# Queries written once and spread into zeroed halves by DMA, with a new table of planning rules, in a fused attention and MLP kernel

## The chip, the cores and the metric

The kernel runs on one core of one Trainium2 chip. The metric is device time in microseconds for one execution. The kernel before has a median of 776.76 us over three runs (775.57 to 777.45).

## The reference, cut to what matters

Two branches read the same x of 2048 rows by 512 columns and are mixed by a gate per row. Branch A is attention with 32 heads of 16 columns. Branch B is an MLP with two layer norms and a shift of four column groups along the rows.

```python
def _A_ref(x, wqkv, wo):                      # B=1, S=2048, D=512, H=32, Dh=16
    q, k, v = split(x @ wqkv)
    scores = jnp.einsum("bhqd,bhkd->bhqk", q, k) * (Dh ** -0.5)
    o = jnp.einsum("bhqk,bhkd->bhqd", _softmax(scores), v)
    return merge(o) @ wo
def _B_ref(x, w1, w2, w3, w4):
    x1 = x + shifted(_gelu(_layernorm(x) @ w1)) @ w2
    return x1 + _gelu(_layernorm(x1) @ w3) @ w4
g = _sigmoid((x * gate_w).sum(-1, keepdims=True))
return g * a + (1 - g) * b
```

The exponentials of the scores are most of the work: 32 heads of 2048 x 2048.

## The kernel before, in words

**Tiles.** Queries are taken in four chunks c of 512 columns (CH). The heads go in eight units u of four heads for each chunk, 32 units in all. A unit holds 64 score blocks: 16 tiles of 128 keys times four heads, and one block is 128 keys by 512 queries. That makes 2048 blocks.

**Queries and the mask.** One product with wq gives a tile ps_q of 128 rows: eight heads of 16 rows, that is two units. A score product takes 32 rows, the keys of two neighbouring heads. So that only one of the two counts, the query tile qT has two halves, each [128, 512]: half a keeps the rows of the heads with number a in their pair, and has zeros in the other rows. In `q_proj` (line 313) the tile is made by one VectorE product of ps_q, read twice, with a mask column for each half (line 321). The mask also holds the factor QS. There are 16 such tiles; the first, for chunk 0 and heads 0 to 7, is made in four pieces at the start (lines 1350 to 1373), the other 15 at line 321.

**Two ways to an exponential.** A score block goes one of two ways. On the first, two or three blocks stand in one PSUM tile `stage`, and ScalarE turns them into probabilities `pt` in one instruction (line 1076, in `expo`). On the second, VectorE dumps a block from the PSUM tile `dsc` as 16-bit integers (line 959, in `whole`), and four blocks of one key tile, a group, are then shifted four times as integers (VectorE line 1000, or GpSimd line 998). The five integer tiles, read as bf16, add up to the exponential. TensorE then multiplies the probabilities with V (line 1089, in `attend_block`), once for a block of the first way, five times for one of the second, and sums in `acc`. The tiles of the second way are named quad, more or xT, after the buffers that they stand in.

**The end of a unit.** `finish_unit` (line 1164) copies acc to the single buffer `accsb` (VectorE, line 1171), moves the denominators by a DMA (den, line 1179), takes reciprocals (line 1186), writes them to DRAM and reads them back spread over rows (rec_d and bcs, lines 1187 and 1188), multiplies on GpSimd (oT, line 1201), and copies the result's rows into a dense tile by four DMAs (line 1210). All these DMAs stand on SyncE's queue (SP), which takes them one by one in the order in which they are written down.

**What sets the order.** The program is a planner that is run when the kernel is built: it keeps a clock of its own for each engine, and writes the instructions down in the order in which they come by that clock. `wants_whole` decides before each score tile whether a block goes to VectorE. Its limits come from `rule`, which looks in a table RULES for the current unit: NEED and AHEAD (how near the end of a unit the next one may start), DLIM (how much VectorE may have waiting), CHAINS (groups open at once), MAXD (the most score blocks of a unit that may go to VectorE). PTS and MANY decide when products with V go ahead of other products. Where TensorE has nothing to do by that clock, `fill` writes products with zeros.

**The last unit.** Its end is cut into ranges of query tiles, j = 0 and 1, j = 2, j = 3. For each j, `out` (line 1290) makes the product with wo. For j = 0 ScalarE and then GpSimd finish the tile (lines 1306 and 1309), for the others VectorE does (line 1299). In the list of TensorE's waiting work a lower number goes first.

Of the kernel before, what the change touches and what calls it, by code (L numbers as in the profile page):

```python
# [12 lines left out]
ALU = mybir.AluOpType  # L13
AX = mybir.AxisListType
BF16 = mybir.dt.bfloat16
# [17 lines left out]
def kernel(  # L33
# [13 lines left out]
    nc = tc.nc  # L47
    P = 128
# [4 lines left out]
    DH = D // H  # L53
# [3 lines left out]
    PTB = 6  # L57
# [5 lines left out]
    CH = 512  # L63
# [18 lines left out]
    qpool = ctx.enter_context(tc.tile_pool(name="qpool", bufs=2))  # L82
# [9 lines left out]
    ptE = young.enter_context(tc.tile_pool(name="ptE", bufs=8))  # L92
# [72 lines left out]
    MM = 0.214  # L165
# [49 lines left out]
    def dma(t, own, count=1):  # L215

        state["sp"] = max(state["sp"], t) + own * count
        return state["sp"]
# [80 lines left out]
    def k_proj(G, c):  # L299
        yield all_at(("xT", c), ("wk", G > 0))  # L300
        ps = gen("ps_k")
        yield from proj(ps, wkv, slice(G * P, (G + 1) * P), xT[c])

        def fn(end):
            nc.vector.tensor_copy(out=kT[G][:, c, :], in_=ps[:])
            at["k", G, c] = end

        evac(0.69, fn)
        yield MM

    qTs = {}

    def q_proj(c, G):
        yield all_at(("xT", c), ("wq", G > 0), ("qfree", NU // 2 * c + G - 2))
        ps = gen("ps_q")
        yield from proj(ps, wq, slice(G * P, (G + 1) * P), xT[c])

        def fn(end):
            qT = qpool.tile([P, 2, CH], BF16, tag="qT", name="qT")
            qTs[(c, G)] = qT  # L320
            nc.vector.tensor_tensor(out=qT[:], in0=ps[:].unsqueeze(1).to_broadcast([P, 2, CH]),
                                    in1=mask[:].unsqueeze(2).to_broadcast([P, 2, CH]), op=ALU.mult)
            at["q", c, G] = end

        evac(1.23, fn)
        yield MM
# [703 lines left out]
    def exp_option():  # L1030
        while next_slot["exp"] in lone:
            next_slot["exp"] += 1
        k = next_slot["exp"]
        if k not in scored:
            return None
        t = scored[k]
        if k in turn:
            return turn[k][2]() if turn[k][1] else t
        back, used = (8, young_pts) if k < EARLY else (PTB, late_pts)
        if len(used) >= back:  # L1040
            if used[-back] not in pt_free:
                return None
            t = max(t, pt_free[used[-back]])
        return t
# [482 lines left out]
```

## Time and profile before

| | before |
|---|---|
| median of three runs | 776.76 us |
| the profiled execution's own time | 777.28 us |
| its span, first to last instruction | 775.5 us |
| mean granted TensorE clock | 0.996 |
| exponentials on ScalarE (line 1076) | 687 |
| score dumps of 512 columns from dsc on VectorE (line 959) | 475 |
| shifts on GpSimd (line 998) | 105 |

The page gives the busy time of each engine, the chain of work that ended last, and groups of instructions by line. A group's row reads: line, engine, operation, tiles, shapes, count, then busy time and the mean duration of one in ns, then the idle time of the engine just before them and what ended it. Where instructions of one engine overlap, busy time is less than count times duration. SPq is SyncE's queue of DMAs. In a row of a timeline the first two numbers are the start and the length in us.

### The profile page before, as it was taken

The numbers are of one execution on the slowest core, as the hardware profiler recorded it, in microseconds if no ns is written. First come the engines' busy times: TensorE is split into PE (matmuls) and PEld (weight loads), VectorE is DVE, ScalarE is ACT, GpSimd is POOL, SyncE is SP. The second block draws the span as 40 slices with busy tenths as digits, with TensorE's granted clock in tenths as the row PEclk, the third lists the DMA queues.
The fourth block names the chain that finished last, engine by engine and source line by source line (L and its number), as shares of the span: only waits on it lengthen the run. The fifth ranks groups of instructions, "written<-read, shape, count | busy, mean of one in ns | idle before, by whom it ended". The sixth has DMA issues, their size and how long they took to land.

```text
span 775.5 us, 24000 instructions
## 1 busy us (share of the span) xinstructions
PE 749.0 (97%) x10166; PEld 245.6 (32%) x10166; DVE 718.0 (93%) x1234; ACT 757.7 (98%) x731; POOL 254.3 (33%) x190
## 2 busy tenths in 40 slices
PE   8999999999999999899999999999999999999997
PEld 4334323333333232232223223322332232332233
DVE  5798999999999999899999999999999989999993
ACT  6999999999999999899999999999999999999995
POOL 3221433442313414234442333123323412443420
PEclk9999999999999999999999999999999999999999
DMA  8600012111130005002000013000040000000010
GB/s 209 192 20 17 13 50 64 31 34 42 19 36 19 19 15 127 20 16 47 20 12 27 19 33 44 18 8 19 19 53 21 16 21 25 21 23 19 20 40 28
DMA packets 52307, 29.05 MB, mean 37 GB/s; under 512 B 36712, under 2 KB 47720, under 8 KB 52200
## 3 DMA queue, kind: packets, MB, share of 16 engines
q1 hardware_dynamic: 51240, 27.00, 15.1%
q8 instruction: 79, 1.29, 0.7%
q10 hardware_dynamic: 960, 0.52, 0.2%
q14 instruction: 28, 0.23, 0.1%
HBM read 17.17 MB, written 2.35 MB: 25 GB/s over the span
## 4 chain that ended last, share of the span: by engine, by line
ACT 51%; PE 29%; issue 16%; DVE 2%; DMA 1%; POOL 0%; POOLq 0%; ACTq 0%; DVEq 0%; SPq 0%
ACT pt L1076 47%; PE acc L1089 11%; PE stage L754 9%; PE ps L271 4%; PE ps_y L271 2%; ACT g2T L1053 1%; PE ps_o L271 1%; ACT g2T L1056 1%; ACT hT L1053 1%; DMA bcs<-rec_d 1%; ACT L1053 1%; PE warm L1330 0%; DVE quad L959 0%; DMA rec_d<-rec 0%; DVE quad L1000 0%
## 5 line engine op out<-in xcount | busy, mean ns | idle before, releaser
L1076 ACT ACTIVATE pt<-stage 128x1024 bf16<-128x1024 f32 (+1 forms) x687 | 707.7, 1207 | 4.1 <-PE stage L754 2.6
L754 PE MATMUL stage<-qT,kT 32*128 32x512 bf16 (+1 forms) x1597 | 271.7, 380 | 16.7 <-ACT pt L1076 12.4
L959 DVE TENSOR_SCALAR quad<-dsc 128x512 int16<-128x512 f32 x342 | 227.6, 683 | 13.2 <-PE dsc L754 10.9
L998 POOL TENSOR_SCALAR quad<-quad 128x2048 int16<-128x2048 int16 x71 | 134.9, 1901 | 261.9 <-DVE quad L1000 145.9
L754 PE MATMUL dsc<-qT,kT 32*128 32x512 bf16 x475 | 182.6, 384 | 0.0
L754 PEld LDWEIGHTS <-kT 32*128 32x128 bf16 x2072 | 81.9, 91 | 284.0 <-issue 250.3
L1000 DVE TENSOR_SCALAR quad<-quad 128x2048 int16<-128x2048 int16 x212 | 146.8, 705 | 2.3 <-PE acc L1089 1.9
L1089 PE MATMUL acc<-pt,vp 128*17 128x512 bf16 (+2 forms) x1572 | 147.4, 379 | 1.4 <-DVE accsb L1171 0.7
L1089 PE MATMUL acc<-quad,vp 128*17 128x512 bf16 x1696 | 145.4, 382 | 0.0
L1089 PEld LDWEIGHTS <-vp 128*17 128x17 bf16 (+1 forms) x4072 | 82.7, 89 | 131.1 <-issue 95.5
L271 PE MATMUL ps<-w,g2T 128*32 128x512 bf16 x896 | 70.5, 382 | 0.0
L1201 POOL TENSOR_TENSOR oT<-accsb,bcs 128x512 bf16<-128x512 f32 x29 | 37.1, 1278 | 66.1 <-DVE quad L1000 48.8
L271 PE MATMUL ps_y<-xnT,w 128*32 128x512 bf16 x704 | 56.2, 387 | 1.0 <-DVE accsb L1171 0.8
L959 DVE TENSOR_SCALAR more<-dsc 128x512 int16<-128x512 f32 x77 | 51.2, 681 | 1.8 <-PE dsc L754 1.6
L998 POOL TENSOR_SCALAR more<-more 128x2048 int16<-128x2048 int16 x17 | 32.3, 1900 | 61.2 <-DVE more L1000 31.6
L998 POOL TENSOR_SCALAR xT<-xT 128x2048 int16<-128x2048 int16 x13 | 25.0, 1924 | 69.8 <-DVE quad L1000 31.0
L1089 PE MATMUL acc<-more,vp 128*17 128x512 bf16 x424 | 40.4, 380 | 0.0
L959 DVE TENSOR_SCALAR xT<-dsc 128x512 int16<-128x512 f32 x56 | 37.3, 681 | 2.6 <-PE dsc L754 2.2
L271 PEld LDWEIGHTS <-w 128*32 128x32 bf16 x1152 | 28.0, 96 | 34.3 <-issue 17.2
L1089 PE MATMUL acc<-xT,vp 128*17 128x512 bf16 x380 | 36.0, 383 | 0.0
L271 PE MATMUL acc<-wq,zero 128*32 128x512 bf16 x324 | 29.8, 383 | 0.0
L271 PEld LDWEIGHTS <-g2T 128*32 128x32 bf16 x896 | 19.3, 95 | 22.1 <-issue 14.3
(117 smaller groups left out, 598.4 us busy)
## 6 DMA issues: line engine op xcount, KB each, us to landing
bcs<-rec_d SPq DMA_DIRECT2D x31, 256.0 KB
w<-in_B_w_dram SPq DMA_DIRECT2D x2, 1792.0 KB
out_dram<-ot SPq DMA_DIRECT2D x15, 128.0 KB
x_sb<-in_A_x_dram SPq DMA_DIRECT2D x14, 128.0 KB
oT<-oT SPq DMA_DIRECT2D x112, 16.0 KB
w<-in_B_w_dram SPq DMA_DIRECT2D x2, 512.0 KB
wkv<-in_A_wqkv_dram SPq DMA_DIRECT2D x1, 512.0 KB
wo_all<-in_A_wo_dram SPq DMA_DIRECT2D x8, 64.0 KB
```

The lines of the kernel that those rows point to most:

```text
L271: nc.tensor.matmul(out[j:j + 32, :], lhsT=lhsT[:, j:j + 32], rhs=rhs, tile_position=(0, j), **kwargs)
L754: nc.tensor.matmul(out, lhsT=kT[G][32 * j:32 * j + 32, cc, o:o + P], rhs=qTs[(c, G)][32 * j:32 * j + 32, a, lo:hi], start=True, stop=True, ...
L959: nc.vector.tensor_scalar(out=bits[:, r:r + wide, :], in0=dsc.rearrange("p (a c) -> p a c", c=CH), scalar1=SHIFT, scalar2=LOWEST, op0=ALU. ...
L998: behind(nc.gpsimd.tensor_scalar(out=tiles[to], in0=tiles[base], scalar1=1.0, scalar2=shift, op0=ALU.mult, op1=ALU.add))
L1000: fast["ins"] = nc.vector.tensor_scalar(out=tiles[to], in0=tiles[base], scalar1=shift, scalar2=None, op0=ALU.add)
L1053: nc.scalar.activation(out=part, in_=part, func=ACT.Gelu_apprx_tanh)
L1056: nc.scalar.activation(out=dst, in_=stages.pop(k)[:, 0:len(ms) * CH].rearrange("p (a c) -> p a c", c=CH), func=ACT.Gelu_apprx_tanh)
L1076: nc.scalar.activation(out=pt[:, 0:w], in_=stages.pop(k)[:, 0:w], func=ACT.Exp, scale=LN2 / 128.0)
L1089: nc.tensor.matmul(accs[n][32 * j:32 * j + M, lo:hi], lhsT=lhsT, rhs=p, start=(kt == 0), stop=(kt == NT - 1), skip_group_check=True, tile_ ...
L1201: behind(nc.gpsimd.tensor_tensor(out=oT, in0=tiles["accsb"][:], in1=tiles["bcs"][:], op=ALU.mult))
```

## The change

VectorE now writes the queries once, scaled, into a tile `dense` of [128, 512]. Eight DMAs on SyncE's queue, one for each head, put its 16-row strips into the half that each belongs to. The query tiles are two fixed buffers, qbufs, that take turns. Their other rows stay zero: buffer 1 is cleared by GpSimd at the start, buffer 0 is written with its zeros by the first tile's four pieces. The planner counts the eight DMAs at 0.6 us each, and 2.3 us more, before a score may read the tile. Early pt buffers go from eight to seven. The table RULES differs for 26 of the 31 units that it has; the caps MAXD of units 1 to 31 (20 where a unit names none, and for the last) add up to 540 blocks before and 528 in the change. In the last unit the product of j = 0 goes ahead of other work.

```diff
-    qpool = ctx.enter_context(tc.tile_pool(name="qpool", bufs=2))
+    qpool = ctx.enter_context(tc.tile_pool(name="qpool", bufs=1))
...
-    ptE = young.enter_context(tc.tile_pool(name="ptE", bufs=8))
+    ptE = young.enter_context(tc.tile_pool(name="ptE", bufs=7))
...
-    RULES = {1: {"MANY": 8, "NEED": 32, "WIDE": 1, "AHEAD": 16, "MAXD": 20, "PTS": 6, "CHAINS": 2, "HURRY": 14, "DLIM": 1.2},
+    RULES = {1: {"WIDE": 1, "NEED": 34, "AHEAD": 12, "HURRY": 18, "DLIM": 0.9, "MANY": 8, "PTS": 3, "CHAINS": 6, "MAXD": 16},
...
     qTs = {}
+    qbufs = [const.tile([P, 2, CH], BF16, name=f"qT{i}") for i in range(2)]
+    nc.gpsimd.memset(qbufs[1][:], 0.0)
...
         def fn(end):
-            qT = qpool.tile([P, 2, CH], BF16, tag="qT", name="qT")
-            qTs[(c, G)] = qT
-            nc.vector.tensor_tensor(out=qT[:], in0=ps[:].unsqueeze(1).to_broadcast([P, 2, CH]),
-                                    in1=mask[:].unsqueeze(2).to_broadcast([P, 2, CH]), op=ALU.mult)
-            at["q", c, G] = end
-
-        evac(1.23, fn)
+            dense = qpool.tile([P, CH], BF16, tag="dense", name="dense")
+            nc.vector.tensor_scalar(out=dense[:], in0=ps[:], scalar1=QS, scalar2=None, op0=ALU.mult)
+            qT = qTs[(c, G)] = qbufs[G % 2]
+            for o in range(0, P, DH):
+                nc.sync.dma_start(out=qT[o:o + DH, o // DH % 2, :], in_=dense[o:o + DH, :])
+            at["q", c, G] = dma(end, 0.6, 8) + 2.0 + MARGIN
+
+        evac(0.69, fn)
...
-        back, used = (8, young_pts) if k < EARLY else (PTB, late_pts)
+        back, used = (7, young_pts) if k < EARLY else (PTB, late_pts)
...
-                queue["pe"].append((2 - 3 * r, 2 * MM, lambda begin, j=j: out(j), fits))
+                queue["pe"].append((2 - 3 * r if j else -10, 2 * MM, lambda begin, j=j: out(j), fits))
...
-    qT = qpool.tile([P, 2, CH], BF16, tag="qT", name="qT")
-    qTs[(0, 0)] = qT
+    qT = qTs[(0, 0)] = qbufs[0]
```

The table moves instructions on all engines. Three places are shown. The first is ScalarE at its last exponentials, from some forty of them to the end; "x8" means that eight like it follow one another. Before:

```order
L1076 ACTIVATE pt<-stage 128x1024 x8
L1076 ACTIVATE pt<-stage 128x1536
L1076 ACTIVATE pt<-stage 128x1024 x4
L1076 ACTIVATE pt<-stage 128x1536 x3
L1076 ACTIVATE pt<-stage 128x1024 x8
L1076 ACTIVATE pt<-stage 128x1536 x6
L1076 ACTIVATE pt<-stage 128x512
L1076 ACTIVATE pt<-stage 128x1024 x2
L1076 ACTIVATE pt<-stage 128x1536 x4
```

And ScalarE at the same place of the change:

```order
L1079 ACTIVATE pt<-stage 128x1024 x4
L1079 ACTIVATE pt<-stage 128x1536 x3
L1079 ACTIVATE pt<-stage 128x1024 x12
L1079 ACTIVATE pt<-stage 128x1536 x8
L1079 ACTIVATE pt<-stage 128x1024 x16
L1079 ACTIVATE pt<-stage 128x1536 x8
L1079 ACTIVATE pt<-stage 128x1024 x2
L1079 ACTIVATE pt<-stage 128x1536 x4
```

Wide and narrow exponentials change places here as in most units. Over the whole order there are 511 of 1024 columns, 175 of 1536 and one of 512 before, 491 of 1024 and 194 of 1536 in the change. VectorE's groups of four blocks go from 125 to 121 (500 blocks to 484), and their shifts from 395 on VectorE and 105 on GpSimd to 399 and 85. TensorE's zero products go from 332 to 516.

The second place is SyncE's queue from the first unit's end on. Before:

```order
L1179 DMA den<-accsb 128x1x16
L1187 DMA rec_d<-rec 128x16
L1188 DMA bcs<-rec_d 128x1x512
L1210 DMA oT_252<-oT 16x512 x4
L1179 DMA den<-accsb 128x1x16
L1187 DMA rec_d<-rec 128x16
L1188 DMA bcs<-rec_d 128x1x512
L1210 DMA oT_252<-oT 16x512 x4
L1179 DMA den<-accsb 128x1x16
L1187 DMA rec_d<-rec 128x16
L1188 DMA bcs<-rec_d 128x1x512
```

And SyncE's queue there in the change, with lines three higher:

```order
L1182 DMA den<-accsb 128x1x16
L1190 DMA rec_d<-rec 128x16
L1191 DMA bcs<-rec_d 128x1x512
L325 DMA qT_244<-dense 16x512 x8
L1213 DMA oT_255<-oT 16x512 x4
L1182 DMA den<-accsb 128x1x16
L1190 DMA rec_d<-rec 128x16
L1191 DMA bcs<-rec_d 128x1x512
L1213 DMA oT_255<-oT 16x512 x4
L1182 DMA den<-accsb 128x1x16
L325 DMA qT_243<-dense 16x512 x8
L1190 DMA rec_d<-rec 128x16
```

The first eight query DMAs stand between a unit's bcs and its oT copies, the second eight between a unit's den and its rec_d. The second kind of place is the most frequent of the 15.

The third place is TensorE at the very end, the products of the last unit's ranges. L1263 makes denominators, L1275 spreads reciprocals, and each two products of L1294 make one tile j. Before:

```order
L1275 MATMUL end<-identf,rec 32x128 x8
L1263 MATMUL end<-pick,accsb 128x4
L1275 MATMUL end<-identf,rec 32x128 x8
L1294 LDWEIGHTS oT_256
L1294 MATMUL end<-wo_pad,oT_256 128x512
L1294 LDWEIGHTS oT_257
L1294 MATMUL end<-wo_pad,oT_257 128x512
```

And TensorE's end in the change:

```order
L1266 MATMUL end<-pick,accsb 128x4
L1297 LDWEIGHTS oT_259
L1297 MATMUL end<-wo_pad,oT_259 128x512
L1297 LDWEIGHTS oT_260
L1297 MATMUL end<-wo_pad,oT_260 128x512
L1266 MATMUL end<-pick,accsb 128x4
L1278 MATMUL end<-identf,rec 32x128 x8
L1297 LDWEIGHTS oT_259
```

The tile of j = 0 now stands ahead of the last range's denominators, where before all four tiles stood behind them.

2 lines of the change are left out of this document (1 added, 1 removed).

## The prediction

> **What bounds the kernel now.** I read the busy shares first, then the stretch in which exponentials run, then what the engines waited for.
>
> ```profile
> PE 749.0 (97%) x10166; PEld 245.6 (32%) x10166; DVE 718.0 (93%) x1234; ACT 757.7 (98%) x731; POOL 254.3 (33%) x190
> ACT 51%; PE 29%; issue 16%; DVE 2%; DMA 1%; POOL 0%; POOLq 0%; ACTq 0%; DVEq 0%; SPq 0%
> ```
>
> ScalarE (ACT), TensorE (PE) and VectorE (DVE) are all nearly full, and the chain that ended last runs half over ACT. Which of the three is the floor shows in the busy time between the first exponential (8.68 us) and the end of the last (766.6 us). The first line has all engines (stretch, its length, then busy time of PE, PEld, DVE, ACT, POOL), the second line 1076, the exponential, alone.
>
> ```profile
> 8.68:766.60 757.92, 737.81 (x10066) 239.89 (x10067) 711.63 (x1218) 754.07 (x725) 246.96 (x154) 1.00 0.16 36
> 8.68:766.60 757.92, 707.70 (x687) 1.00 0.16 36
> ```
>
> ACT is busy 754.07 of 757.92 us there, 707.70 in exponentials and 46.4 in GELUs and table loads. Successive exponentials overlap, so the price of one is its pace, from stretches that hold hardly anything but one shape:
>
> ```profile
> L1076 ACT ACTIVATE pt<-stage 128x1024 bf16<-128x1024 f32 x12 | 11.1, 1103 | 0.0
> L1076 ACT ACTIVATE pt<-stage 128x1536 bf16<-128x1536 f32 x5 | 6.9, 1545 | 0.0
> L1076 ACT ACTIVATE pt<-stage 128x1024 bf16<-128x1024 f32 x511 | 482.7, 1101 | 2.3 <-PE stage L754 0.9 <-PE dsc L754 0.7
> L1076 ACT ACTIVATE pt<-stage 128x1536 bf16<-128x1536 f32 x175 | 245.9, 1521 | 1.7 <-PE stage L754 1.7
> ```
>
> Twelve of two blocks in 11.1 us, the last 1.10 long: (11.1 - 1.10)/11 = 0.909 us. Five of three blocks: (6.9 - 1.545)/4 = 1.339 us. At this pace 511 and 175 exponentials, and one of 512 columns (about 0.48), need 464.5 + 234.3 + 0.5 = 699.3 us. So of 757.92 us, 699.3 + 46.4 = 745.7 can't shrink unless ACT gets fewer blocks, and **12.2 us are lost** to late score tiles. ACT is the floor; DVE and PE matter only through these 12.2 us, or through the split of blocks between ACT and DVE.
>
> **The change, part by part.** (1) *The split of the blocks.* The order of before has 511, 175 and 1 exponentials of 1024, 1536 and 512 columns: 1548 of the 2048 score blocks. The order of the change has 491 and 194: 1564. Sixteen blocks, four DVE groups of four, move to ACT. At the pace: 491 x 0.909 + 194 x 1.339 = 446.3 + 259.8 = 706.1 us, so **+6.8 us on the bounding engine**. This rests on counts and two paces alone.
>
> (2) *DVE and POOL.* Rows of before: the masked product, a PSUM evacuation of 512 columns, a score dump, the shifts on DVE and on POOL.
>
> ```profile
> L321 DVE TENSOR_TENSOR qT<-ps_q,mask 128x1024 bf16<-128x1024 f32 x15 | 18.2, 1214 | 0.3 <-PE ps_q L271 0.3
> L305 DVE CAST kT<-ps_k 128x512 bf16<-128x512 f32 x15 | 10.2, 683 | 4.6 <-PE ps_k L271 4.4
> L959 DVE TENSOR_SCALAR quad<-dsc 128x512 int16<-128x512 f32 x342 | 227.6, 683 | 13.2 <-PE dsc L754 10.9
> L1000 DVE TENSOR_SCALAR quad<-quad 128x2048 int16<-128x2048 int16 x212 | 146.8, 705 | 2.3 <-PE acc L1089 1.9
> L998 POOL TENSOR_SCALAR quad<-quad 128x2048 int16<-128x2048 int16 x71 | 134.9, 1901 | 261.9 <-DVE quad L1000 145.9 <-DVE more L1000 40.8 <-DVE xT L1000 20.5
> ```
>
> Fifteen products become fifteen dense writes, which I price as the evacuation of line 305: 15 x (1.214 - 0.683) = 8.0 us less. Sixteen dumps fewer: 10.9 less. Shifts: DVE 395 before and 399 in the change, POOL 105 and 85: DVE +2.8 us, POOL -38.0. DVE in all about 16 us less, 718 to 702. None of it counts by itself, since ACT is fuller; it counts only if it shortens the 12.2 us. Work is taken off the two engines with room and put on the one without.
>
> (3) *PE.* A DVE block is multiplied with V five times over, an ACT block once, so sixteen blocks moved are 64 products, 16 passes of four strips, less. Three passes take 0.83 us, the last 0.39 of it, so (0.83 - 0.39)/2 = 0.22 us each: 3.5 us less. The order also has more zero products that only occupy PE: 332 before (324 into acc, 8 spare), 516 in the change: 46 passes, 10.1 us. They stand where the planner saw PE without work, so I cost them at nothing; badly placed, each delays a score by 0.22.
>
> ```profile
> 313.03 0.83 PE L271 MATMUL ps_y<-xnT,w 128*32 128x512 bf16 x12
> PE stage L754 <- ACT pt L1076: 12.4, 52, 0.8
> PEld L754 <- DVE quad L959: 12.2, 32, 0.5
> ```
>
> What comes of the lost time? PE waits for ACT 52 times but for a dump only 32 times, and a score is late mostly because other passes stand ahead of it. Counted over PE's order at 0.22 us a pass and some 0.1 for each turn between scores and other work, the zero products apart, the work from one score to the next exceeds its exponential's pace in 201 places before and in 180 in the change, a tenth fewer. I take **1 us less**. Bounds: the loss may fall to some 4 us (8 less) if the lighter DVE also ends most waits for dumps, or rise by the third rival.
>
> (4) *The eight DMAs.* Nearest rows: the row copies of oT, same 16x512 shape, and SP's wait for a small write to land.
>
> ```profile
> L1210 SPq DMA_DIRECT2D oT<-oT x112: 555/582/1739, 55.1 to 741.0; - x112
> SPq L1188 <- DMA rec_d<-rec: 39.9, 31, 2.8
> ```
>
> Eight issues take 8 x 0.582 = 4.7 us of SP, landing some 1.3 us (39.9/31) after the last, so queries are ready some 6 us after the dense write where they were ready at the product's end. By PE's order the first score on the new queries stands 7 to 15 exponentials after the last ps_q matmul, at 0.9 to 1.3 us each: 6.4 us at the tightest against 0.7 + 6.0. I take nothing; if all fifteen were as tight as the tightest, each would cost about 0.3, 4.5 in all. The 15 x 4.7 = 70 us of SP time lie on a queue that mostly waits; what they block is the third rival. The Trainium skill (DMA: Bandwidth & Descriptors, Rules for kernel authors) speaks against this part: transfers under 64 KB are mostly overhead and should be joined. The row of 0.58 us for 16 KB agrees, 28 GB/s. By that rule the eight cost 4.7 us each time against 0.5 saved on DVE, 62 us in all if nothing hid them; by the exponentials between write and use, nothing.
>
> (5) *The small parts.*
>
> ```profile
> 1.38 0.95 POOL L127 MEMSET vp<- 128x1024 bf16 x1
> 19.41 0.20 POOL L382 TENSOR_SCALAR rstd<-mv 128x4 f32<-128x4 f32 x1 [12.39 <-DVE mv L372]
> ```
>
> The zeroing of qT1 is one memset like the first row, 0.95 us, ahead of a POOL instruction that waits 12.39 us: free. Seven pt buffers instead of eight: in the first 34 slots a tile is read up by the time four more scores are issued, so free; a stall there would be one exponential, 0.9.
>
> (6) *The end.*
>
> ```profile
> 769.51 2.07 DVE L1299 SCALAR_TENSOR_TENSOR ot<-end,g_fin,parts 128x512 bf16<-128x512 f32 x3
> 770.76 0.69 ACT L1306 ACTIVATE ot<-end,g_fin 128x512 f32<-128x512 f32 x1 [3.36 <-PE end L1294]
> 771.53 1.26 POOL L1309 TENSOR_TENSOR ot<-ot,parts 128x512 bf16<-128x512 f32 x1 [24.42 <-ACT ot L1306]
> 772.82 0.33 SPq L1310 DMA_DIRECT2D out_dram<-ot  x1
> ```
>
> Tile j=0 goes the long way, ACT, POOL, store, and was the last to start. Put first it leaves the end; then DVE's third gate, done at 771.58, is late next, and its store can go out some 0.4 later, about 772.0 instead of 772.82. The early product delays the last range by up to two passes, 0.4. **0.8 us less**; bounds 0.4 more to 1.2 less.
>
> Sum: +6.8 - 1.0 - 0.8 = **+5.0 us** on the profiled execution's 777.28, 782.3. That execution ran 0.5 us above the median of 776.76, so I forecast 781.8.
>
> **Rivals.** *First: ACT is fed better and the loss pays for the blocks.* For it: less DVE work, more room on PE, and the 1.7 us lost in the group of rows below may not come again. Against it: even with the loss down to 4 us (8.2 less) the sum is 776.76 + 6.8 - 8.2 - 0.8 = 774.6. It decides from 5.0 us of further gain on. 774 to 778.
>
> *Second: queries come late.* PE takes instructions in order, so one late qT row stops scores for both ACT and DVE. Priced above: up to 4.5 us, 786.
>
> *Third: the eight issues delay the normalisation.* In SP's order most groups of eight stand between a unit's den copy and its rec_d and bcs. The accsb buffer is single, so the next unit's copy waits for POOL's oT, PE's sums wait for that copy, and PE runs dry. Before shows this once in full:
>
> ```profile
> DVE accsb L1171 <- POOL oT L1201: 3.1, 3, 1.5
> 321.39 0.69 DVE L1171 COPY accsb<-acc 128x512 f32<-128x512 f32 x1 [1.46 <-POOL oT L1201]
> 322.13 1.41 PE L271 MATMUL ps_y<-xnT,w 128*32 128x512 bf16 x12 [0.85 <-DVE accsb L1171]
> 325.04 1.45 ACT L1076 ACTIVATE pt<-stage 128x1536 bf16<-128x1536 f32 x1 [1.51 <-PE stage L754]
> 326.70 1.02 ACT L1076 ACTIVATE pt<-stage 128x1024 bf16<-128x1024 f32 x1 [0.21 <-PE dsc L754]
> 320.00:327.00 7.00, 6.08 (x69) 1.97 (x72) 4.68 (x9) 5.28 (x5) 2.37 (x2) 0.76 0.06 13
> ```
>
> The copy was 1.46 us late, PE idle 0.85, the granted clock fell to 0.76 over these seven microseconds, and ACT was busy 5.28 of 7.00: 1.7 us lost. It costs nothing while oT is done before the next copy's turn; that slack is gone in three units already (the 3 of the first row), and 4.7 us more on SP use it up in others; two to four more such places are 3.4 to 6.8 us, 785 to 789. Against it: DVE's lighter load lets the reciprocal start sooner. The Trainium skill (TensorE: Matmul & The Clock Gate, Part 1) says that the clock halves after an idle window of some 3.4 us and recovers after a busy one. The row of 0.76 over seven microseconds agrees with about one such window, but PE had idled only 0.85 us at a stretch ahead of it; by the rule's words the clock would have stayed up, each such place would cost PE's own 0.85, and two to four of them 1.7 to 3.4; the measured 1.7 each stands.
>
> **How the numbers follow.** Forecast as worked out (779 to 784): 0.60. First rival: 0.22, half of it under 775.2. Second 0.04, third 0.14. A measurement of this kernel can tell some 0.2%, 1.55 us, from no change. Faster, under 775.2: half of the first rival, 0.11. Same, 775.2 to 778.3: the rest of it and the forecast's lowest edge, 0.14. Slower: 0.75. The range, 776 to 788, leaves out most of the first rival and the far end of the third.
>
> **What would show it.** Right: 685 exponentials at the same paces, ACT busy some 7 us longer, DVE near 702, the loss between 8 and 13 us, POOL's last add ahead of DVE's last gate. Wrong: a stretch of exponentials no longer than 758 us (first rival), scores waiting for a DMA of qT (second), or more waits of accsb for oT with a granted clock under 1 behind them (third). A pace of exponentials under 0.9 us would break the main term.

## The result, and the profile after

| | before | changed |
|---|---|---|
| median, us | 776.16 (775.09 to 777.45) | 787.3 (785.47 to 787.97) |
| ratio | 1 | 1.0141, 95% interval 1.0127 to 1.0154 |
| profiled execution, us | 777.28 | 787.97 |
| its span, us | 775.5 | 786.2 |
| first exponential to end of the last, us | 757.92 | 769.39 |
| of that not covered by exponentials' pace, GELUs, table loads | 12.2 | 17.0 |
| end of the last exponential to end of span, us | 8.9 | 7.8 |

The change costs 11 us. The forecast was 5.0 more on the profiled execution; it is 10.7 more.

The page of the changed kernel, busy shares and the shares of the chain that ended last:

```profile
PE 758.1 (96%) x10286; PEld 251.1 (32%) x10286; DVE 709.5 (90%) x1219; ACT 764.4 (97%) x729; POOL 219.6 (28%) x171
ACT 45%; PE 34%; issue 13%; DVE 5%; DMA 2%; SPq 1%; POOL 0%; DVEq 0%; POOLq 0%; ACTq 0%
```

VectorE and GpSimd lost work (8.5 and 34.7 us), ScalarE and TensorE gained some (6.7 and 9.1). In the chain the share of ACT fell and those of PE, DVE and DMA rose: the exponentials wait more. The stretch of the exponentials, all engines and then the exponential's line alone (columns as in the prediction), and the two shapes of exponentials:

```profile
9.05:778.44 769.39, 746.70 (x10200) 244.86 (x10201) 703.06 (x1203) 760.80 (x723) 211.34 (x134) 1.00 0.17 38
9.05:778.44 769.39, 714.45 (x685) 1.00 0.17 38
```

```profile
L1079 ACT ACTIVATE pt<-stage 128x1024 bf16<-128x1024 f32 x491 | 465.2, 1110 | 7.6 <-PE dsc L757 4.0 <-PE acc L1092 2.5 <-PE stage L757 0.7
L1079 ACT ACTIVATE pt<-stage 128x1536 bf16<-128x1536 f32 x194 | 270.8, 1543 | 1.2 <-PE stage L757 1.1
```

The counts are those forecast. 491 x 0.909 + 194 x 1.339 = 706.1 us of pace, and 760.80 - 714.45 = 46.3 us of ScalarE's other work, leave 769.39 - 706.1 - 46.3 = 17.0 us lost. So of the 10.7 us, 6.8 are the pace of 16 more blocks, **4.7 are a larger loss** (16.95 less 12.24 before rounding) where 1.0 less was forecast, 0.4 lie ahead of the first exponential, and the end gives back 1.1. Where the loss is shows in the waits (sum, count, longest), first of the changed kernel and then of before:

```profile
ACT pt L1079 <- PE dsc L757: 4.0, 5, 2.7
ACT pt L1079 <- PE acc L1092: 2.5, 5, 0.9
DVE accsb L1174 <- POOL oT L1204: 2.0, 1, 2.0
ACT pt L1079 <- PE stage L757: 1.8, 4, 0.6
```

```profile
ACT pt L1076 <- PE stage L754: 2.6, 5, 1.5
ACT pt L1076 <- PE dsc L754: 0.7, 3, 0.3
```

The second row is new. An exponential that is released by a product *into acc* had its scores; what it lacked was a free buffer for its probabilities, which the product of an older buffer with V gave back. Before has no such wait. With a seventh buffer these waits are gone (below), so this reading holds. One of the five places, from the timeline (start, length, then the wait in brackets):

```profile
524.58 0.83 PE L1092 MATMUL acc<-pt,vp 128*17 128x512 bf16 x12
525.07 2.37 ACT L1079 ACTIVATE pt<-stage 128x1024 bf16<-128x1024 f32 x2 [0.91 <-PE acc L1092]
```

The three passes of the first row are the late products; since the copy of the old sum at 518.99 ten passes with integer tiles were taken ahead of them. At 385.77 and 719.02 passes with integer tiles stand ahead too, and the exponential starts 6 to 7 us behind such a copy; at 448.82 and 651.8 other products, of the output and of the MLP, stand ahead.

The third row of the waits, and most of the first, are one place, the prediction's third rival, at 199 to 208 us:

```profile
199.24 1.26 POOL L1204 TENSOR_TENSOR oT<-accsb,bcs 128x512 bf16<-128x512 f32 x1 [4.80 <-DMA bcs<-rec_d]
200.54 0.69 DVE L1174 COPY accsb<-acc 128x512 f32<-128x512 f32 x1 [2.05 <-POOL oT L1204]
201.28 1.05 PE L271 MATMUL ps_y<-xnT,w 128*32 128x512 bf16 x8 [2.05 <-DVE accsb L1174]
202.97 2.10 ACT L1079 ACTIVATE pt<-stage 128x1024 bf16<-128x1024 f32 x2 [2.67 <-PE dsc L757]
205.56 1.02 ACT L1079 ACTIVATE pt<-stage 128x1024 bf16<-128x1024 f32 x1 [0.49 <-PE dsc L757]
207.07 2.37 ACT L1079 ACTIVATE pt<-stage 128x1024 bf16<-128x1024 f32 x2 [0.48 <-PE dsc L757]
```

```profile
199.00:208.00 9.00, 6.95 (x59) 1.33 (x58) 5.84 (x10) 5.29 (x7) 1.26 (x1) 0.62 0.04 10
```

Read it downward: GpSimd waits 4.80 us for bcs, the end of the chain den, reciprocal, rec_d, bcs; the copy of the next sum waits 2.05 us for GpSimd; TensorE, next in line, stands for 2.05 us; its clock is granted at 0.62 over these nine microseconds; and the exponentials wait 2.67, 0.49 and 0.48. ScalarE is busy 5.29 of 9.00 us: 3.7 lost, against 1.7 at before's one place of this kind. These 2.0 more and the 2.5 of the buffers are 4.5 of the 4.7.

Why bcs is late stands on SyncE's queue. Between this unit's den and its rec_d it has the eight issues and, behind them, four transposing DMAs of xn:

```profile
179.96 5.40 SPq L325 DMA_DIRECT2D qT<-dense  x8
185.46 5.16 SPq L407 DMA_TRANSPOSE xnT<-xn  x4
190.72 1.69 SPq L1190 DMA_DIRECT2D rec_d<-rec  x1
```

The reciprocal is done at 186.34; its rec_d starts 4.4 us later.

### The profile page after: what moved, and what is told of

Same layout as the page of the kernel before. It is cut to its first block, busy times and chain, and to the rows that moved or that the text cites. A ratio compares the mean times of both kernels' runs of the same rounds, so it can differ in the third digit from the quotient of the medians.

```text
span 786.2 us, 24376 instructions
## 1 busy us (share of the span) xinstructions
PE 758.1 (96%) x10286; PEld 251.1 (32%) x10286; DVE 709.5 (90%) x1219; ACT 764.4 (97%) x729; POOL 219.6 (28%) x171
## 4 chain that ended last, share of the span: by engine, by line
ACT 45%; PE 34%; issue 13%; DVE 5%; DMA 2%; SPq 1%; POOL 0%; DVEq 0%; POOLq 0%; ACTq 0%
ACT pt L1079 42%; PE acc L1092 12%; PE stage L757 10%; PE ps L271 5%; DVE quad L962 2%; PE ps_y L271 1%; PE stage L271 1%; PE ps_o L271 1%; PE ps_q L271 1%; ACT g2T L1056 1%; DVE quad L1003 1%; SPq L407 1%; ACT hT L1056 1%; DMA xnT<-xn 1%; DMA bcs<-rec_d 1%
## 5 line engine op out<-in xcount | busy, mean ns | idle before, releaser
L757 PE MATMUL stage<-qT,kT 32*128 32x512 bf16 (+2 forms) x1617 | 272.3, 381 | 17.3 <-ACT pt L1079 11.7
L962 DVE TENSOR_SCALAR quad<-dsc 128x512 int16<-128x512 f32 x330 | 219.3, 684 | 19.4 <-PE dsc L757 17.2
L757 PE MATMUL dsc<-qT,kT 32*128 32x512 bf16 x455 | 176.0, 387 | 0.0
L1001 POOL TENSOR_SCALAR quad<-quad 128x2048 int16<-128x2048 int16 x53 | 102.4, 1932 | 258.8 <-DVE quad L1003 191.3
L1003 DVE TENSOR_SCALAR quad<-quad 128x2048 int16<-128x2048 int16 x216 | 152.4, 719 | 4.9 <-PE acc L1092 4.6
L962 DVE TENSOR_SCALAR xT<-dsc 128x512 int16<-128x512 f32 x69 | 45.9, 684 | 7.1 <-PE dsc L757 6.8
L1001 POOL TENSOR_SCALAR more<-more 128x2048 int16<-128x2048 int16 x13 | 24.7, 1897 | 79.5 <-DVE quad L1003 48.6
L271 PE MATMUL acc<-wq,zero 128*32 128x512 bf16 x496 | 46.3, 387 | 0.0
L962 DVE TENSOR_SCALAR more<-dsc 128x512 int16<-128x512 f32 x56 | 37.2, 684 | 2.8 <-PE dsc L757 2.4
L1092 PE MATMUL acc<-xT,vp 128*17 128x512 bf16 x368 | 35.8, 381 | 0.0
```

The source lines that it names most:

```text
L271: nc.tensor.matmul(out[j:j + 32, :], lhsT=lhsT[:, j:j + 32], rhs=rhs, tile_position=(0, j), **kwargs)
L757: nc.tensor.matmul(out, lhsT=kT[G][32 * j:32 * j + 32, cc, o:o + P], rhs=qTs[(c, G)][32 * j:32 * j + 32, a, lo:hi], start=True, stop=True, ...
L962: nc.vector.tensor_scalar(out=bits[:, r:r + wide, :], in0=dsc.rearrange("p (a c) -> p a c", c=CH), scalar1=SHIFT, scalar2=LOWEST, op0=ALU. ...
L1001: behind(nc.gpsimd.tensor_scalar(out=tiles[to], in0=tiles[base], scalar1=1.0, scalar2=shift, op0=ALU.mult, op1=ALU.add))
L1003: fast["ins"] = nc.vector.tensor_scalar(out=tiles[to], in0=tiles[base], scalar1=shift, scalar2=None, op0=ALU.add)
L1092: nc.tensor.matmul(accs[n][32 * j:32 * j + M, lo:hi], lhsT=lhsT, rhs=p, start=(kt == 0), stop=(kt == NT - 1), skip_group_check=True, tile_ ...
```

## The experiments

The theory that I went in with had two parts: ScalarE's pace carries the split of blocks (+6.8), and the rest comes from two waits, the buffers' and the one behind SyncE's issues. Its rivals were that the DMAs cost more than this, or that the order, not the number of blocks, is what is dear.

### The two halves of the change apart: order and DMAs

The change's order, instruction for instruction, with the masked product in place of the dense write and its DMAs:

```diff
-            dense = qpool.tile([P, CH], BF16, tag="dense", name="dense")
-            nc.vector.tensor_scalar(out=dense[:], in0=ps[:], scalar1=QS, ...)
...
-            for o in range(0, P, DH):
-                nc.sync.dma_start(out=qT[o:o + DH, ...], in_=dense[o:o + DH, :])
+            nc.vector.tensor_tensor(out=qT[:], in0=ps[:]..., in1=mask[:]..., op=ALU.mult)
```

> Every instruction stands as in the change, but VectorE makes the masked product straight into the two fixed query buffers and the 120 query DMAs are gone; VectorE has 8 us more. Theory A with all loss from the order: no faster than the change, 786 to 790. Theory A with part of the loss from SyncE's queue (normalisation late, clock halved): 781 to 784, with the wait of accsb for oT of 2 us gone and no scores at half clock near 203 us. Theory B: back at 776 to 778.

Measured: 785.22 us, ratio 1.0110 (1.0095 to 1.0125), between the two forms of theory A and far from theory B. And before's order with the dense write and the 120 DMAs (the memset and the seven early buffers too), which is the same edit the other way round:

> Every instruction stands as in before, but the 15 products are dense writes and the 120 DMAs go out behind them; 1548 blocks on ScalarE. First scores on new queries stand 3 to 12 exponentials behind the last ps_q matmul, and queries need some 6.7 us. If late queries stop TensorE: shortfalls of about 1.2 us in four places and 3.3 in two, 11 us, so 785 to 789 with scores waiting for a DMA of qT. If DMAs only matter through the order: 775 to 778.

Measured: 807.45 us, ratio 1.0396 (1.0381 to 1.0412): late queries do stop TensorE, at 18 us above the upper end that was expected for them. The four cases side by side:

| | masked product | dense write, eight DMAs |
|---|---|---|
| before's order | 776.16 | 807.45 |
| the change's order | 785.22 | 787.3 |

In the change's order the DMAs cost 2.1 us, and the order costs 9.0 without them (8.7 by the 776.57 of before beside that run). In before's order the DMAs cost 31. The timeline and the waits of that kernel show why:

```profile
390.55 0.69 DVE L322 TENSOR_SCALAR dense<-ps_q 128x512 bf16<-128x512 f32 x1 [0.32 <-PE ps_q L271]
393.05 4.97 SPq L325 DMA_DIRECT2D qT<-dense  x8
397.52 0.37 PE L757 MATMUL dsc<-qT,kT 32*128 32x512 bf16 x1 [3.77 <-DMA qT<-dense]
```

```profile
ACT pt L1079 <- PE dsc L757: 28.1, 17, 5.6
PE dsc L757 <- DMA qT<-dense: 15.3, 5, 3.9
```

The dense write starts at 390.55, SyncE gets to its first issue at 393.05, and TensorE, in order, stands at a score dump for 3.77 us until the rows are there at 397.52. Five such places make 15.3 us of TensorE's waits and 25.5 of the exponentials' 28.1. Behind each of the five the granted clock is 0.50 for 3.4 or 6.8 us, 27.3 in all, which the expectation hadn't counted. That is the second rival. It doesn't occur in the changed kernel, where no score waits for a DMA of qT; so the new order has the DMAs' room, and its price, 9 us, is most of the change's loss. Whether another order would give that room for less, no run shows.

In the change's order with the product, the place at 199 us is gone and the wait for buffers is not:

```profile
196.25 10.23 ACT L1077 ACTIVATE pt<-stage 128x1024 bf16<-128x1024 f32 x10
196.57 1.26 POOL L1202 TENSOR_TENSOR oT<-accsb,bcs 128x512 bf16<-128x512 f32 x1 [2.00 <-DVE xn L392]
198.24 0.68 DVE L1172 COPY accsb<-acc 128x512 f32<-128x512 f32 x1
```

```profile
ACT pt L1077 <- PE acc L1090: 2.8, 7, 0.9
```

Without the issues the four transposes start at 178.64 instead of 185.46 and rec_d at 186.49 instead of 190.72. oT comes at 196.57 instead of 199.24, 2.5 us sooner by the exponentials there, which run 0.17 sooner; the copy waits for nothing, and ten exponentials run through. By the starts of the same exponentials in both traces 4.2 us are gained at this place, and 1.1 of them are gone again later. The third rival's place comes from the eight issues; the buffers' waits come from the order.

### The tables crossed

The change's code with before's table of rules (480 exponentials of 1024 columns, 205 of 1536, 1 of 512):

> The change with the table RULES of before; its order gives ScalarE 480 exponentials of 1024 columns, 205 of 1536 and one of 512, 1576 blocks. Theory A (time follows the blocks left to ScalarE, and the table decides them): exponentials at the paces 0.909 and 1.339 us need 711.3 us, 12.0 more than before; with the loss of before 788, with the loss of the change 792. Theory B (the DMAs cost the time, the table little): as the change, 785 to 788.

Measured: 808.55 us, ratio 1.0415 (1.0399 to 1.043). Both theories were over 16 us too low. And before's code with the change's table (491 and 198 exponentials):

> The kernel before with the table RULES of the change, so the masked product and no query DMAs; 491 and 198 exponentials, 1576 blocks. Theory A: 711.4 us of exponentials, 788 to 792, slower than the change although it has none of its DMAs. Theory B: without the DMAs it is near before, 776 to 781.

Measured: 812.33 us, ratio 1.0463 (1.0445 to 1.048), 20 us above theory A. Each table belongs to the code that it came with: 32 or 36 us for crossing them. Of each, 12 are the pace of 28 more blocks; the loss is 32.4 and 35.8 us where before's is 12.2, and waits for buffers alone are 17.2 and 21.1 of it. My reading, which no run separates from others, is that the costs that the planner is given for a query (0.69 us and eight issues, or 1.23) shift its order everywhere, so that the rules of one unit meet another situation. What such an order loses shows before's code with the change's table at the turn from one unit to the next:

```profile
433.49 1.48 PE L271 MATMUL acc<-wq,zero 128*32 128x512 bf16 x24
441.40 0.68 DVE L1171 COPY accsb<-acc 128x512 f32<-128x512 f32 x1
442.14 0.40 PE L1089 MATMUL acc<-pt,vp 128*32 128x512 bf16 x4 [0.54 <-DVE accsb L1171]
442.63 2.37 ACT L1076 ACTIVATE pt<-stage 128x1024 bf16<-128x1024 f32 x2 [9.65 <-PE acc L1089]
```

From 433.49 on TensorE multiplies zeros between the old unit's last integer terms, which VectorE delivers one by one. Until the old sum is copied out at 441.40, the new unit's probabilities have no accumulator; they fill all six buffers, and ScalarE stands for 9.65 us. It is the wait for a buffer of the changed kernel's five small places at a far greater size; of those five only the one at 448.82 stands within 2 us of the copy of a sum.

### A seventh buffer for probabilities

If the buffers' 2.5 us are a price of their own, one more buffer takes it away, with the order as it is. The room was found in two ways. First by one shared buffer for output rows and dense queries, a narrower tile of zeros and the identity in a buffer of oT (the lines shown are those of the pools):

```diff
-    ptpool = ctx.enter_context(tc.tile_pool(name="pt", bufs=PTB))
+    ptpool = ctx.enter_context(tc.tile_pool(name="pt", bufs=PTB + 1))
-    otp = ctx.enter_context(tc.tile_pool(name="otp", bufs=2))
+    otp = ctx.enter_context(tc.tile_pool(name="otp", bufs=1))
```

> The change with seven pt buffers after the early part instead of six, paid for by sharing other buffers; the order of all compute instructions is unchanged. Theory (ScalarE waits for a free pt buffer in five or more places, 2.5 to 3.3 us): those waits are gone and the time is 784 to 785. Rival (those places are late for another reason, and the wait moves to the score): 787.

Measured: 789.24 us, ratio 1.0166 (1.0152 to 1.018). The waits for buffers are gone, but the single output buffer stalls once for its store (DVE for out_dram 3.0 us, TensorE behind it 2.7), so the time tells nothing. The same in the change's code with before's table, where the wait is large:

> The change with the table of before and seven pt buffers; with six ScalarE waited 17.2 us for products that free a pt buffer, in nine places. Theory: some 15 us come back, 791 to 794, near 711.3 us of exponentials plus the loss of before. Rival (the products are late for lack of V sums or VectorE's terms, and one more buffer only delays the wait): 802 to 808.

Measured: 812.48 us, ratio 1.0467 (1.0451 to 1.0483), against 808.55 with six. The waits for buffers fell from 17.2 to 8.6 us, those for dsc rose from 1.8 to 8.9 and those for stage from 3.2 to 5.6: they moved, though the time lies above the rival's range too. The single output buffer stalls this kernel as well, 2.9 us once, so the two aren't separated. Then in the change again, with output rows and dense queries in the pool of xn, five buffers instead of four:

```diff
-    xnpool = ctx.enter_context(tc.tile_pool(name="xn", bufs=4))
+    xnpool = ctx.enter_context(tc.tile_pool(name="xn", bufs=5))
-            dense = qpool.tile([P, CH], BF16, tag="dense", name="dense")
+            dense = xnpool.tile([P, CH], BF16, tag="xn", name="dense")
-                ot = otp.tile([P, CH], BF16, tag="ot", name="ot")
+                ot = xnpool.tile([P, CH], BF16, tag="xn", name="ot")
```

> The changed kernel with seven buffers for probabilities instead of six, order unchanged; the room is paid by letting the dense queries and the output rows share five xn buffers, so that no single buffer is waited for. Theory (a sum that closes late holds all six buffers and stops ScalarE): the waits of an exponential for acc products, 2.5 us, shrink to under 0.5 and the time falls by 1.5 to 3, to 784.3 to 785.8. Rival (the lateness is at the ends of the units, one more buffer only moves the wait to the scores): those waits go, waits for dsc or stage rise by as much, 786.5 to 788.

Measured: 789.75 us, ratio 1.018 (1.0163 to 1.0197): neither. One store again held a buffer that was due:

```profile
461.02 0.75 DVE L558 SCALAR_TENSOR_TENSOR ot<-ps_o,g_fin,x_sb 128x512 bf16<-128x512 f32 x1 [3.32 <-DMA out_dram<-ot]
463.45 1.45 ACT L1078 ACTIVATE pt<-stage 128x1536 bf16<-128x1536 f32 x1 [2.96 <-PE stage L756]
523.73 5.23 ACT L1078 ACTIVATE pt<-stage 128x1024 bf16<-128x1024 f32 x5
```

The last row is the place of 525.07 above, now without a wait. Comparing the starts of the same exponential in both traces: ScalarE gains 0.45, 0.70, 1.04, 0.45 and 0.53 us at the five places (0.56 of the second goes back at the next exponential), and loses 4.3 at 463 to 466. So at the five places themselves the price is as read, about 2.6 us net; that it would be gained as a whole was not shown, since each way to make the room cost more than that.

### Sixteen blocks less on ScalarE

The main term by itself: every eleventh wide exponential takes 1024 columns until sixteen are short, and the order stays.

```diff
-        nc.scalar.activation(out=pt[:, 0:w], in_=stages.pop(k)[:, 0:w], ...)
+        wide = w
+        if w == 3 * CH:
+            state["wide"] = state.get("wide", 0) + 1
+            if state["wide"] % 11 == 0 and len(short) < 16 and k not in cut:
+                wide -= CH
+                short.add(k)
+        nc.scalar.activation(out=pt[:, 0:wide], in_=stages.pop(k)[:, 0:wide], ...)
```

> The changed kernel, its order unchanged, in which 16 of the 194 wide exponentials take 1024 columns instead of 1536; the exponential of 16 blocks is left out (the products of these take the neighbour block's probabilities instead), everything else is issued as before. Theory (ScalarE's own pace is the floor, and the 16 more blocks of the change cost 16 x 0.43 us): 6.9 less by the difference of the paces 1.339 and 0.909, 779.5 to 781.5. Rival (TensorE or VectorE would take over as the bound at once, so the blocks were not the price): 785 to 787.5, with waits of the exponentials for scores grown by 5 to 7 us.

Measured: 785.75 us, ratio 1.012 (1.0105 to 1.0135), 1.5 us less than the change. Judged by the time, the rival was right: 6.9 us less pace came to about a fifth of that, and the loss rose from 17.0 to 21.5, by 4.5 where 5 to 7 had been named. Nearly every short exponential did let the next one start 0.43 us earlier; but of the last seven's 3.0 us, 0.43 were left at the end. One of them, by TensorE's and ScalarE's share of a stretch from one score to another, first with the short exponential and then the same scores in the change (columns as above; then the exponential behind it):

```profile
684.59:688.49 3.90, 3.90 (x64) 1.26 (x60) 3.20 (x7) 3.66 (x4) 1.90 (x1) 1.00 0.02 2
687.89 2.10 ACT L1087 ACTIVATE pt<-stage 128x1024 bf16<-128x1024 f32 x2 [0.24 <-PE dsc L757]
```

```profile
686.67:690.57 3.90, 3.90 (x62) 1.26 (x59) 3.19 (x7) 3.90 (x4) 1.90 (x1) 1.00 0.02 2
```

The scores lie 3.90 us apart in both, and TensorE is busy for all of it in both, here with useful passes only. ScalarE's 3.90 became 3.66 and a wait of 0.24: the gain is gone. The Trainium skill (Perfetto Trace Analysis, Identifying the Most-Contended Engine) says to take the engine of the highest occupancy first, for TensorE by other measures than its busy share. ScalarE has the highest here, 97%; taking 6.9 us off it gave 1.5, so the measurement goes against the rule where a second engine is this close.

Is it the zero products that fill it up elsewhere? In a second kernel sixteen other wide exponentials are shortened, each chosen where a zero product of four strips stands right behind it, and these sixteen are left out too:

```diff
+    SHORT = (45, 56, 131, 160, 171, 196, 224, 273, 304, 385, 410, 468, 504, 532, 624, 644)
+    GONE = (1, 5, 19, 29, 33, 39, 60, 72, 81, 93, 95, 102, 107, 114, 120, 124)
...
+            if state["fill"] not in GONE:
+                strips(acc[:], lhsT=zero[:], rhs=wq[:, 0, :], ...)
```

> The changed kernel, its order unchanged, in which 16 wide exponentials take 1024 columns instead of 1536 (the exponential of 16 blocks is left out and their products take the neighbour block's probabilities), and behind each of these 16 the next zero product of 4 strips is left out on TensorE, 0.37 us each. The run with 16 short exponentials alone won 1.5 us of the 6.9: each gave 0.43 us, and within some twelve exponentials TensorE had taken it back. Theory (in a fixed order TensorE's stream is cut to the exponentials, filled up with zero products, so that only what is saved on both counts): 16 x 0.37 = 5.9 to 16 x 0.43 = 6.9 less than the change's 787.3, 780.4 to 781.8, and the short exponentials keep their 0.43. Rival (it is TensorE's useful work, or VectorE's gates, that take the gain back, the zero products merely fill idle time): as with the short exponentials alone, 784.5 to 786.5.

Measured: 784.42 us (780.09 to 789.52, wider than any other), ratio 1.011 (1.0079 to 1.014). Judged by the time, it is the lower end of the rival's range, 0.1 below it. The interval is 782.0 to 786.8 us by the 775.91 of before beside it, just above the theory's upper end, and one of the six runs, 780.09, lies below that end. The trace says more. Of the first five short exponentials' 2.15 us, 2.0 are still there at 193 us, as the theory has it. Then the third rival's place takes 1.3 of them:

```profile
199.78 0.69 DVE L1178 COPY accsb<-acc 128x512 f32<-128x512 f32 x1 [3.29 <-POOL oT L1208]
201.84 2.10 ACT L1082 ACTIVATE pt<-stage 128x1024 bf16<-128x1024 f32 x2 [3.54 <-PE dsc L757]
```

The chain of DMAs didn't become shorter with the exponentials; everything else came to it earlier, and the copy waits 3.29 us where it waited 2.05. Of the other eleven's 4.7 us, 1.95 were left at the end. So the gain of a freed ScalarE goes to TensorE's stream, useful passes and zero products alike, and to latencies that don't shrink. The two kernels shorten different exponentials, so what the sixteen zero products bring by themselves was not separated.

### The eight issues on GpSimd's queue

If SyncE's queue is what makes the place at 199 us, the issues can go elsewhere:

```diff
-                nc.sync.dma_start(out=qT[o:o + DH, o // DH % 2, :], in_=dense[o:o + DH, :])
+                nc.gpsimd.dma_start(out=qT[o:o + DH, o // DH % 2, :], in_=dense[o:o + DH, :])
```

> The changed kernel with the queries' eight DMAs issued by GpSimd's queue instead of SyncE's, order unchanged. Theory (eight issues in a row on SyncE hold up rec_d of the normalisation, accsb stays taken, TensorE runs dry once and its clock halves): the wait of 2.0 us of DVE for oT and the half-speed matmuls behind it are gone, 784.5 to 785.7, as with the product in the same order (785.2). Rival (the issues cost GpSimd as much as they cost SyncE, and its adds and oT products come later): other waits on GpSimd's results take their place, 786.5 to 790.

Measured: 799.94 us, ratio 1.0314 (1.0285 to 1.0342). The theory was right at its place, where by the exponentials' starts 4.2 us are gained between 199.8 and 203.5, and wrong in sum: the rival's waits come, and the time is 10 us beyond its own range. The group of the issues, and one of the places:

```profile
L325 POOL DMA_DIRECT2D qT<-dense x120 | 72.9, 615 | 59.0 <-DVE dense L322 52.8 <-ACT g_t L438 6.0
```

```profile
421.28 4.68 POOL L325 DMA_DIRECT2D qT<-dense  x8 [2.86 <-DVE dense L322]
427.95 0.61 PE L1092 MATMUL acc<-xT,vp 128*17 128x512 bf16 x4 [3.04 <-POOL xT L1001]
428.67 0.69 DVE L1174 COPY accsb<-acc 128x512 f32<-128x512 f32 x1 [3.37 <-PE acc L1092]
429.73 1.45 ACT L1079 ACTIVATE pt<-stage 128x1536 bf16<-128x1536 f32 x1 [2.58 <-PE acc L1092]
```

GpSimd waits 2.86 us for the dense write, issues for 4.68, and the shift of xT behind it is 3.04 us late for TensorE; the sum closes late, and an exponential waits 2.58 us for a buffer. On SyncE only DMAs stand behind an issue; on GpSimd the terms of the sums do. But such waits are not all. Of the 15.0 us by which this profiled execution, the slowest of four, is longer than the change's, 6.3 lie behind the last exponential. The last stores leave SyncE as in the change:

```profile
791.61 0.99 SPq L1304 DMA_DIRECT2D out_dram<-ot  x2
```

From their end to the end of the span are 8.6 us here and 2.3 in the change; what the program does in them the views don't show. VectorE's shifts take longer in this kernel too; the commonest form, first with the issues on GpSimd and then in the change:

```profile
L1003 DVE TENSOR_SCALAR quad<-quad 128x2048 int16<-128x2048 int16 x216 | 163.3, 770 | 4.8 <-PE acc L1092 4.5
```

```profile
L1003 DVE TENSOR_SCALAR quad<-quad 128x2048 int16<-128x2048 int16 x216 | 152.4, 719 | 4.9 <-PE acc L1092 4.6
```

0.770 us instead of 0.719; VectorE is busy 11.0 us longer in all. The single shifts tell more than the mean. Of all 399, five take 2.6 to 4.4 us; each begins during an issue and ends 0.55 us after the GpSimd instruction that follows the issues. One of them, where GpSimd's next shift runs from 724.27 to 726.18:

```profile
723.58 3.15 DVE L1003 TENSOR_SCALAR quad<-quad 128x2048 int16<-128x2048 int16 x1
```

The 68 shifts that run beside issues and no other GpSimd instruction take 0.69 us on average and 0.71 at most. In the change twelve shifts take over 0.9 us, 2.4 at most, all beside a GpSimd instruction. The Trainium skill (SBUF — State Buffer, Who interferes with whom) has GpSimd write the descriptors of its DMAs through ports that it shares with some of VectorE's operations; beside the issues alone no shift shows such a wait here.

### The tail's edit alone

The change without the edit that puts tile j=0 first:

> The change without its last edit: the product of tile j=0 stands behind the last range again. Theory (0.8 us as predicted): 788.1. Rival (the early product delays the last range by as much as it gains): 787.3, no difference.

Measured: 787.1 us, ratio 1.0142 (1.0127 to 1.0158). Its instructions stand in the same order as the change's on TensorE: by the change's table the tile's product stood there already, so the edit does nothing in the change, and this is a second measurement of it. Its profiled execution lost 15.8 us in the exponentials where the change's lost 17.0, which is how far two executions of one order differ. Before with the edit alone:

```diff
-                queue["pe"].append((2 - 3 * r, 2 * MM, lambda begin, j=j: out(j), fits))
+                queue["pe"].append((2 - 3 * r if j else -10, 2 * MM, lambda begin, j=j: out(j), fits))
```

> The kernel before with that edit alone: j=0 first, all else as before. Theory: 0.8 to 1.1 us faster than before, 775.5, and so faster than both kernels; POOL's last add is over before VectorE's last gate. Rival: no difference.

Measured: 775.18 us in five rounds, against 776.23 of before beside it, ratio 0.9986 (0.9977 to 0.9995). The span ends 8.0 us after the last exponential instead of 8.9. In this profiled execution TensorE's clock is never halved between the first exponential and the last, in before's it is once, so a part of the medians' difference may be that. This is the fastest kernel of the study: one line of the change, without the rest.

## Why the prediction came out as it did

The time lies in the range, slower as forecast, and 5.5 us above the forecast. It is outside the forecast as worked out, 779 to 784, and inside the third rival's 785 to 789, though that rival's place came once and not two to four times. So the range held by the room that it left for a rival, and in part by luck. Of the signs of being right the 685 exponentials, ScalarE's 6.7 us and GpSimd's early last add came; VectorE at 709.5 instead of 702 and a loss of 17.0 instead of 8 to 13 did not. One slip in the chances: the one of the same time counts an edge of the forecast below 778.3, and the forecast begins at 779. By its steps:

1. *The split of the blocks, +6.8.* The counts hold, and ScalarE is busy 6.7 us longer. The sentence under it fell: "ACT is the floor; DVE and PE matter only through these 12.2 us". With sixteen blocks less on ScalarE alone, 1.5 us came back. In this order TensorE's stream is as full as ScalarE's, and at the place shown above both are floors from one exponential to the next. The 6.8 are in the time, but they are a price of the order that holds them, which costs 9.0 without the DMAs, and not one that ScalarE alone could pay back.
2. *VectorE, GpSimd, TensorE at nothing.* Fifteen dense writes took 10.2 us, 0.682 each, as priced; VectorE fell by 8.5 instead of 16, in part because its shifts took 7.4 us more where 2.8 were counted, the slow ones beside GpSimd; TensorE rose by 9.1, where -3.5 and 10.1 of zero products were counted. No gain from any of it, as forecast.
3. ***The loss, 1.0 less: the step that failed.*** It was counted as TensorE's passes standing ahead of scores. It was 4.7 more. Outside the buffers' places and the third rival's 0.2 more were lost where 1.0 less was forecast, a difference as large as the 1.2 by which two executions of this order differ. But a score's being early isn't enough for an exponential. It needs a free buffer for its probabilities as well, and the new order puts the products that free one so late that five exponentials wait, 2.5 us, which before never did. This wait was in none of the rivals. The other 2.0 are the third rival's place, which the forecast put at nothing.
4. *The eight DMAs at nothing in the forecast.* No score waits for them, and an issue takes 0.580 us where 0.582 was priced, but they cost 2.1 us through the third rival, which came in one place, with 3.7 us lost where before's one place lost 1.7. The order with the masked product has no such place. The third rival asked for two to four; the mechanism was right and its count too high. It named the groups of eight between a den and its rec_d: eight of the fifteen stand so, and none of them made such a place. The one that did has the four transposes of xn between den and rec_d as well. The second rival, given 0.04, is real in the other order: 31 us, seven times its price of 4.5. That price was for the change's order with at least seven exponentials between write and use; before's order has three to twelve, a late queue stops TensorE for up to 3.9 us and not for 0.3, and the clock is halved behind each stop.
5. *The small parts.* The memset took 0.956 us and delayed nothing; the first wait for a buffer comes at 385 us, so the early ones don't matter.
6. *The end, 0.8 less.* It was 1.1 less, by the mechanism given; from the changed kernel's trace:

```profile
779.75 0.69 ACT L1309 ACTIVATE ot<-end,g_fin 128x512 f32<-128x512 f32 x1 [0.49 <-PE end L1297]
780.52 1.27 POOL L1312 TENSOR_TENSOR ot<-ot,parts 128x512 bf16<-128x512 f32 x1 [5.89 <-ACT ot L1309]
781.44 2.07 DVE L1302 SCALAR_TENSOR_TENSOR ot<-end,g_fin,parts 128x512 bf16<-128x512 f32 x3 [0.15 <-PE end L1297]
782.87 0.99 SPq L1304 DMA_DIRECT2D out_dram<-ot  x2
```

   GpSimd is done at 781.79, ahead of VectorE's third gate at 783.51, and the stores of the gates go last. The line that does this isn't the edit, though, which changes nothing here; in before's order it is, and is worth about 1 us: 1.05 by the medians, 0.9 at the end of the span.

What stays open: of the order's 9.0 us, 2.5 are the buffers'; how the rest divides between ScalarE's blocks and TensorE's passes was not settled, since taking away one left the other in its place.

## What to carry to other kernels

In an order that a planner packs, find the floor from one step to the next, not by the sum over the kernel: here two engines at 97 and 96% were both the floor, and most of the work taken off one alone came back as a wait for the other. When a short product is replaced by a chain with a latency, ask for the price of the order that makes room for the latency; here the DMAs cost 2 us, the order with room for them 9, and doing without the room 31. Where a queue takes its DMAs in order, count everything that stands between two DMAs of one chain; the place that cost most had eight issues and four transposes there. And count for each instruction of the bounding engine where its *output* goes: a full set of output buffers stopped it here as a late input did.

## What the runs showed of the hardware

TensorE's clock fell after less idling than expected. In the changed kernel TensorE stood for 2.05 us ahead of 201.28, and the granted clock was 0.50 from 200.41 to 207.24, so from 1.2 us into that stretch on. In the 3.41 us up to 200.41 TensorE was busy for 1.57. In before the clock was 0.50 from 322.25 to 325.66; TensorE had stood twice, for 0.83 and 0.85 us, and was busy for 1.74 of the 3.41 us up to 322.25. The Trainium skill (TensorE: Matmul & The Clock Gate, Part 1) has the clock halve after an idle window of some 3.4 us; here windows that were about half idle were enough. The length of one stretch doesn't decide it: 1.27 us ahead of 309.84 in the changed kernel, and 1.70 ahead of 149.39 in before's order with the DMAs, left the clock at 1.00.

Moving an issue from SyncE to GpSimd didn't make it cheaper: 0.599 us in the middle on GpSimd (0.615 on average) against 0.580 in the middle on SyncE (0.608 on average), from the changed kernel's row of DMA issues:

```profile
L325 SPq DMA_DIRECT2D qT<-dense x120: 507/580/1692, 46.9 to 718.5; - x120
```
